# Attention with q/k norms, then a two-layer MLP: one swap of two VectorE steps, wider score groups in two units, one MLP item earlier in two others, two edits in the opening

## The chip, the cores and the metric

The kernel runs on one core of one Trainium2 chip. The metric is the device time of one execution in microseconds (us). A core has TensorE (PE in the profile, its weight loads PEld), VectorE (DVE), ScalarE (ACT), GpSimd (POOL) and SyncE (SP, which here only issues DMAs). Each engine runs its own instructions in the order in which the program recorded them; what ties them together are semaphores.

## The reference

q, k and v have 8 batches, 12 heads, 448 rows and 64 columns. The result goes through a two-layer MLP ("MoE" in the code) of 768 by 2048 and 2048 by 768.

```
q_n = q / sqrt(mean(q*q) + 1e-6) * g_q          # the same for k with g_k
scores = 1/8 * q_n @ k_n.T
attn = exp(scores - max(scores)); attn = attn / (sum(attn) + 1e-9)
x = (attn @ v), heads side by side: 3584 x 768
h = x @ w_in;  g = max(0.01*h, h);  out = g @ w_out
```

## The kernel before, in words

**Units.** The attention is cut into 24 units: unit u holds 4 heads of one batch, so a batch is three units. The 448 rows of a head are 7 tiles of 64, and the scores are computed transposed: for one of the seven steps t, four matmuls of 64x64 by 64x448 (L222) fill a pair of PSUM banks (a "slot"). ScalarE turns a slot into exponentials in one pass of 128x896 (`ex`, L242), which frees the slot. After the seven steps come attn @ v (`pv`, L398) and the column sums (`zcol`, L335).

**The shift in front of exp.** It comes from the first score tile of a unit: VectorE takes its maximum (L262), spreads it over a diagonal tile `dg` (L264), TensorE multiplies that by ones (L274, or L280 in the first units), VectorE reduces again (L275) and writes the bias `eb` (L285). Only then can the unit's first exp run.

**Four stages per unit.** In the main loop each unit has stages d = 0 to 3. Before, units 3 to 6 follow `STEPS`: one score step at d = 0 and two at each of the others. Units 7 to 21 follow `TRIPLES`: one at d = 0, three at d = 1, none at d = 2, three at d = 3 (`tripled(u)`, L780). Between the score groups TensorE runs items of the MLP out of one queue. How many are taken at each stage is written out by hand in `PLAN`, a string of four digits for each unit from unit 3 on (L774). An item is one tile of the first layer (`moe1`: 6 matmuls at L420, then ScalarE's activation L414, which frees its bank), half of a plain second-layer tile (`moe2`: 16 matmuls in two parts, L466, copied out by VectorE at L473), or one of seven products (`seven`, 8 matmuls each, L516). `seven` computes two output tiles with seven products instead of eight; its parts are merged by VectorE additions (L523).

**Who goes first on VectorE.** `fill` (L789) takes an item, then pops one job from the stage's list, and so on; `flush` runs what an item put off with `later`: copies, additions, and the `drop` of a bank. Jobs are steps that prepare later units: sums of squares (L180), 1/rms on ScalarE (L185, L186), the norm itself (`prep_norm`, two multiplications at L192, q and k), the transposition by DMA (L209), the scaling of the transposed q (L176), sums of weights for the seven products (L491). One exception is written out: in unit 12 no job follows the item that is marked `merges`.

**Banks.** PSUM has 8 banks. `aux` hands out one, `slot` a pair; as a rule the bank or pair that has been free the longest is taken (once all are shared, a single bank is taken first from a pair whose other half is in use), and its next matmul waits until the last reader of the previous use is done. Before unit 7 banks 0 to 3 are single ones and 4 to 7 make the two slots; from unit 7 on (`shared`, L1025) all eight are one pool.

**The opening.** Units 0 to 2 are written out line by line (L820 to L1021). TensorE runs matmuls without a use (`warm`, L817) where it would stand idle. Two places matter: 48 of them ahead of unit 0's transpositions (L832), and the bank `st[2]["pb"]`, held from the shift of unit 2 until after the transposition of q for unit 3 (`trn(3, 0)`, L986; `drop` at L988). `trn` transposes seven 128x128 tiles on TensorE (L204) into one single bank, and VectorE copies them out (L801 for q, L803 for k).

Of the kernel before, what the change touches and what calls it, by code (L numbers as in the profile page):

```python
# [18 lines left out]
def kernel(  # L19
# [18 lines left out]
    NU = B * NQ  # L38
# [25 lines left out]
    def aux():  # L64
        can = [i for i in free if mine(i)]
        if shared:
            can = [i for i in can[:-1] if i ^ 1 not in free] or can
        free.remove(can[0])
        return single[can[0]]
# [12 lines left out]
    def drop(tile_):  # L82
        for i in range(8):
            if tile_ is single[i]:
                assert i not in free
                free.append(i)
                return
        x = [i for i in range(4) if tile_ is double[i]][0]
        assert 2 * x not in free and 2 * x + 1 not in free
        free.extend((2 * x, 2 * x + 1))  # L90
# [42 lines left out]
    st = {}  # L133
# [33 lines left out]
    def prep_sq(u, c=ALL, tis=BOTH):  # L167
        for ti in tis:
            nc.scalar.activation(buf(u, f"sq{ti}")[:, :, c[0]:c[1]], raw[u][ti][:, :, c[0]:c[1]], AF.Square)  # L169
# [29 lines left out]
    def prep_tr(u, ti, copies):  # L199
        bank = aux()  # L200
        tp = as_tp(bank)
        for (lo, hi), copy in copies:
            for x in range(lo, hi):
                nc.tensor.transpose(tp[:, x, :], buf(u, "n16")[:, ti, x].rearrange("p a d -> p (a d)"), ident16)  # L204
            copy(buf(u, "qkT")[:, ti, lo:hi], tp[:, lo:hi], ti == 0)
        drop(bank)
# [25 lines left out]
    def ex(u, most=NS):  # L232
        s = st[u]
        if "et" not in s:
            s["et"] = epool.tile([P, NS, 2, S], FP16, tag="et", name="et")
        for t, sT in s["sT"][:most]:
            if isinstance(sT, list):
                for a in range(2):
                    nc.scalar.activation(s["et"][:, t, a], sT[a][:, 0:S], AF.Exp, bias=s["eb"], scale=1.0)  # L239
                    drop(sT[a])  # L240
            else:
                nc.scalar.activation(s["et"][:, t], sT[:, :, 0:S], AF.Exp, bias=s["eb"], scale=1.0)  # L242
                drop(sT)
        s["sT"] = s["sT"][most:]
# [189 lines left out]
    def store(pair, t, tile_, c, last):  # L434
        for y in range(2):
            n = 2 * t + (1 - y if t < 3 else y)
            b, grp = 2 * pair + n // NS, n % NS
            dst = out[b * S:(b + 1) * S, :].rearrange("(p t) m -> p t m", t=NS)
            eng = nc.scalar if last and y else nc.sync
            eng.dma_start(dst[:, grp, c], tile_[64 * y:64 * y + 64, c])  # L440
# [5 lines left out]
    def flush(keep=0):  # L446
        kept = [p for p in pend if keep and (p[0] in (s1, s2, s3, s4) or hasattr(p[0], "waits") or keep == 5 and hasattr(p[0], "copies"))]
        now = [p for p in pend if p not in kept]
        pend[:] = kept
        for fn, args in now:  # L450
            fn(*args)

    def out_tile():
        return opool.tile([P, DM], FP32, tag="ost", name="ost")
# [29 lines left out]
    def wblock(i, j):  # L484
        return wout16[:, HF * i:HF * i + HF, HC * j:HC * j + HC]
# [7 lines left out]
    def gblock(t, j):  # L493
        return gt[:, HF * j:HF * j + HF, ds(col(t), P)]
# [13 lines left out]
    def later(fn, *args):  # L508
        pend.append((fn, args))

    def seven(pair, tt, nxt=None, last=False, mixed=False):
        g = {}

        def mm(bank, a, b, first, fs=range(HF)):
            for f in fs:
                nc.tensor.matmul(bank[:, 0:HC], a[:, f], b[:, f], start=(first and f == 0), stop=(f == HF - 1), skip_group_check=not first)  # L516

        def bank(name):
            g[name] = aux()
            return g[name]  # L520

        def add(dst, src, name):
            nc.vector.tensor_tensor(dst, g[name][:, 0:HC], src, op=ALU.add)  # L523

        def put(i, c):
            store(pair, tt[i], g["o"][i], c, last)

        def i0():
            flush()
            g["o"] = (out_tile(), out_tile())  # L530
            ma = bank("ma")
            if mixed:
                mm(ma, gblock(tt[0], 0), wblock(0, 0), True, range(6))
                mm(bank("mb"), sa[:, 1], tw[:, 1], True, range(4))
            mm(ma, gblock(tt[0], 0), wblock(0, 0), True, range(6 if mixed else 0, HF))
            if mixed:
                mm(bank("mc"), sa[:, 0], tw[:, 0], True, range(4))
            later(lambda: nc.vector.tensor_copy(g["o"][1][:, L], g["ma"][:, 0:HC]))

        def i1():  # L540
            flush()
            mm(g["mb"] if mixed else bank("mb"), sa[:, 1], tw[:, 1], True, range(4 if mixed else 0, HF))
            later(lambda: add(g["o"][1][:, L], g["o"][1][:, L], "mb"))
            later(lambda: drop(g["mb"]))

        def i2():
            flush()
            mm(g["ma"], gblock(tt[0], 1), wblock(1, 0), False)
            later(lambda: nc.scalar.copy(g["o"][0][:, L], g["ma"][:, 0:HC]))
            later(lambda: drop(g["ma"]))  # L550
            if last:
                later(put, 0, L)

        def i3():
            flush()
            mm(g["mc"] if mixed else bank("mc"), sa[:, 0], tw[:, 0], True, range(4 if mixed else 0, HF))
            later(lambda: add(g["o"][1][:, R], g["o"][1][:, L], "mc"))
            if nxt:
                later(s1, nxt)

        def i4():
            flush()
            mm(bank("md"), sa[:, 2], tw[:, 2], True)
            later(lambda: add(g["o"][1][:, R], g["o"][1][:, R], "md"))
            if last:
                later(put, 1, R)

        i4.merges = True

        def i5():  # L570
            flush()
            mm(g["mc"], sa[:, 3], wblock(1, 1), False)
            if nxt:
                later(s2, nxt)
            later(lambda: add(g["o"][0][:, R], g["o"][1][:, L], "mc"))
            later(lambda: drop(g["mc"]))
            later(put, 0, R if last else LR)
            if nxt:
                later(s3, nxt)
                later(s4, nxt)  # L580

        def i6():
            flush()
            mm(g["md"], gblock(tt[1], 1), tw[:, 3], False)
            def end():
                add(g["o"][1][:, L], g["o"][1][:, L], "md")
                drop(g["md"])
                put(1, L if last else LR)

            end.waits = True  # L590
            later(end)

        return [i0, i1, i2, i3, i4, i5, i6]

    HK = KT // 2
# [133 lines left out]
    def push(b):  # L729
# [32 lines left out]
        else:  # L762
# [9 lines left out]
        queue.extend(items)  # L772

    PLAN = ("2122", "1222", "2112", "2122", "3232", "3322", "2322",  # L774
            "2322", "3232", "2222", "3323", "3232", "2322", "2322",
            "3232", "2222", "3323", "3232", "2322", "4356", "5232")
    STEPS = ((0,), (1, 2), (3, 4), (5, 6))
    TRIPLES = ((0,), (1, 2, 3), (), (4, 5, 6))

    def tripled(u):  # L780
        return 7 <= u < NU - 2

    def narrow(u):
        return 3 <= u < NU - 1
# [4 lines left out]
    def fill(u, d, jobs):  # L789
        for n in range(int(PLAN[u - 3][d])):  # L790
            fn = queue.pop(0)[1]
            fn()
            if jobs and not (d == 2 and u == 12 and hasattr(fn, "merges")):
                jobs.pop(0)()
        flush(keep=u if d == 3 and u < NU - 1 else 0)
        for job in jobs:
            job()
# [17 lines left out]
    def warm(n, bank):  # L815
        for x in range(n):
            nc.tensor.matmul(bank[:, P:2 * P], onesp, onesp, start=True, stop=True)  # L817

    with tc.manual_schedule():
# [7 lines left out]
        wbank = aux()  # L827
# [1 line left out]
        for a in range(2):  # L829
            nc.vector.scalar_tensor_tensor(gdup[:, a], grow[:, 0], 0.125, grow[:, 1], op0=ALU.mult, op1=ALU.mult)  # L830
        nc.tensor.matmul(gps[:, 0:1], gdup.rearrange("o a d -> o (a d)"), one32, start=True, stop=True)
        warm(48, wbank)  # L832
        prep_sq(0, CA, (0,))
        prep_sq(0, CB, (0,))
        prep_sq(0, ALL, (1,))
# [44 lines left out]
        def trn(u, ti, copy):  # L880
            prep_tr(u, ti, ((ALL, copy),))
# [101 lines left out]
        warm(12, st[2]["pb"])  # L983
        qk(2, (3,))
        ex(2)
        trn(3, 0, vcopy)  # L986
        warm(8, st[2]["pb"])
        drop(st[2]["pb"])  # L988
        trn(3, 1, vcopy)
        xmul(1)  # L990
        prep_ssq(4, ALL, (1,))
# [30 lines left out]

        for u in range(3, NU):
            for d in range(4):
                if u == 7 and d == 0:  # L1025
                    shared.append(u)
                if d > 0 or u > 3:
                    qk(u, (TRIPLES if tripled(u) else STEPS)[d])
# [22 lines left out]
                jobs = []  # L1051

                def job(fn, *args):
                    jobs.append(lambda: fn(*args))
# [69 lines left out]
        for i, more in enumerate((((xmul, NU - 1, (1,)), (x_sum, B - 1, 3), (x_sum, B - 1, 1)), ((x_sum, B - 1, 2), (x_sum, B - 1, 4)))):  # L1124
            c, fn = queue[i]
# [33 lines left out]
```

## Time and profile before

| | us |
|---|---|
| median of 3 runs (lowest, highest) | 412.99 (412.83, 414.09) |
| the profiled execution's own time | 412.78 |
| its span, from the first to the last instruction | 411.0 |
| TensorE busy in the span | 395.8 (96%) |
| VectorE busy | 308.7 (75%) |
| ScalarE busy | 299.6 (73%) |
| TensorE busy from 0 to 50 us | 41.4 of 50 |

The profile describes one execution. "Busy" counts the time in which at least one instruction of the engine is in work; matmuls are pipelined, so a matmul that waits a little between others can hide in a busy stretch. The chain that ended last is followed back from the last instruction: at each step to what released it. The view of waits sums, for each engine and line, how long it sat idle and who released it. The timeline lists start, duration, engine, line and operation in order of time, with a bracket for the idle time just before and its releaser. The granted TensorE clock was 0.998 over the span.

### The profile page before, as it was taken

Reading aid. Unit: us, or ns where it says so; the run is one execution under the profiler, and the core shown is the slowest. Engines: PE = TensorE matmul, PEld = TensorE weight load, DVE = VectorE, ACT = ScalarE, POOL = GpSimd, SP = SyncE. Lnnn points to the kernel's source line nnn. Section 1 sums busy time; section 2 is a strip of 40 time slices with the busy share of each in tenths; the row PEclk is TensorE's granted clock in tenths of the full one; section 3 lists DMA queues with packets and bytes.
Section 4 is the critical chain, followed back from the end, with each engine's and each line's share of the span. In section 5 each row is a group of like instructions: output and inputs, shape, how many; then the busy total and the mean of one; then the engine's idle time right before and its main releaser. Section 6 shows DMA issues by size and latency. Waiting matters only on the chain.

```text
span 411.0 us, 9411 instructions
## 1 busy us (share of the span) xinstructions
PE 395.8 (96%) x3840; PEld 223.8 (54%) x3840; DVE 308.7 (75%) x490; ACT 299.6 (73%) x470; POOL 69.3 (17%) x70
## 2 busy tenths in 40 slices
PE   8688999999999999999999999999999999999996
PEld 7455454455455544555454554555455557558963
DVE  5997789998888765867678766778578888657672
ACT  5998977677978599778877689868985667753600
POOL 1787332200020200020020200002011202000000
PEclk9999999999999999999999999999999999999999
DMA  6999999999565985578566996677652460032023
GB/s 201 263 238 253 236 235 239 229 194 195 140 155 97 242 216 105 148 195 179 147 157 69 224 203 132 156 147 193 176 98 46 121 154 15 10 77 77 2 52 102
DMA packets 72526, 62.87 MB, mean 153 GB/s; under 512 B 36388, under 2 KB 67620, under 8 KB 72484
## 3 DMA queue, kind: packets, MB, share of 16 engines
q1 hardware_dynamic: 61888, 50.08, 47.5%
q0 software_dynamic: 10272, 11.80, 18.4%
q8 instruction: 30, 0.49, 0.5%
q10 hardware_dynamic: 324, 0.39, 0.3%
q14 instruction: 12, 0.10, 0.1%
HBM read 45.61 MB, written 11.01 MB: 138 GB/s over the span
## 4 chain that ended last, share of the span: by engine, by line
PE 86%; DVE 6%; ACT 5%; issue 1%; DMA 1%; DVEq 0%; ACTq 0%
PE banks L420 28%; PE banks L516 22%; PE banks L222 9%; PE banks L466 8%; PE banks L398 7%; PE banks L648 6%; ACT et L242 3%; PE banks L335 3%; PE banks L817 2%; DVE n L192 1%; DMA out_dram<-ost 1%; PE banks L274 1%; PE banks L204 1%; DVE xt L407 1%; ACT et L239 1%
## 5 line engine op out<-in xcount | busy, mean ns | idle before, releaser
L242 ACT ACTIVATE et<-banks,eb 128x896 f16<-128x896 f32 x166 | 160.3, 1014 | 29.2 <-PE banks L222 16.9
L420 PE MATMUL banks<-xt,win 128*128 128x448 f16 x612 | 122.2, 353 | 0.0
L420 PEld LDWEIGHTS <-win 128*128 128x128 f16 x612 | 57.3, 98 | 55.8 <-issue 6.5
L414 ACT ACTIVATE gt<-banks 128x448 f16<-128x448 f32 x104 | 56.6, 564 | 6.3 <-PE banks L420 5.2
L222 PE MATMUL banks<-qkT 64*64 64x448 f16 x672 | 50.7, 362 | 4.5 <-ACT et L242 3.4
L180 DVE TENSOR_REDUCE ssq<-sq 128x14 f32<-128x896 f32 (+2 forms) x49 | 50.2, 1058 | 0.5 <-ACT sq L169 0.5
L516 PE MATMUL banks<-tw,sa 128*128 128x384 f16 x264 | 46.8, 326 | 2.0 <-DVE ost L523 2.0
L516 PEld LDWEIGHTS <-sa 128*128 128x128 f16 x352 | 33.5, 98 | 26.5 <-issue 5.5
L149 POOL DMA_DIRECT2D vt<-in_v_dram x24 | 17.9, 748 | 166.2 <-PE banks L398 165.8
L523 DVE TENSOR_TENSOR ost<-banks,ost 128x384 f32<-128x384 f32 x55 | 30.4, 553 | 16.1 <-PE banks L516 15.0
L222 PEld LDWEIGHTS <-qkT 64*64 64x64 f16 x672 | 17.8, 104 | 35.4 <-issue 28.6
L398 PE MATMUL banks<-et,vt 64*64 64x448 f16 x672 | 37.0, 349 | 0.1
L516 PEld LDWEIGHTS <-gt 128*128 128x128 f16 x264 | 25.5, 98 | 18.0 <-issue 1.4
L466 PE MATMUL banks<-wout,gt 128*128 128x384 f16 x192 | 34.1, 327 | 0.0
L376 POOL TENSOR_TENSOR xt<-x,rz 128x896 f16<-128x896 f32 x9 | 19.7, 2190 | 80.7 <-DMA rz<-zs 73.2
L262 DVE TENSOR_REDUCE banks<-banks 128x1 f32<-128x896 f32 x22 | 24.1, 1097 | 12.0 <-PE banks L222 8.8
L516 PE MATMUL banks<-wout,gt 128*128 128x384 f16 x176 | 32.4, 326 | 0.0
L350 ACT COPY x<-banks 128x896 f32<-128x896 f32 x16 | 14.5, 907 | 22.7 <-DVE banks L275 22.7
L192 DVE TENSOR_TENSOR n<-rq,rinv 128x896 f16<-128x896 f32 (+2 forms) x25 | 27.1, 1089 | 1.6 <-ACT rinv L186 1.6
L192 DVE TENSOR_TENSOR n<-rk,rinv 128x896 f16<-128x896 f32 (+2 forms) x26 | 27.5, 1065 | 0.0
L398 PEld LDWEIGHTS <-vt 64*64 64x64 f16 x672 | 20.3, 107 | 10.6 <-issue 0.4
L466 PEld LDWEIGHTS <-gt 128*128 128x128 f16 x192 | 17.7, 98 | 13.8 <-issue 3.2
(103 smaller groups left out, 468.5 us busy)
## 6 DMA issues: line engine op xcount, KB each, us to landing
rq<-in_q_dram SPq DMA_DIRECT2D x24, 448.0 KB, 4.1
rk<-in_k_dram SPq DMA_DIRECT2D x24, 448.0 KB, 4.6
out_dram<-ost SPq DMA_DIRECT2D x52, 192.0 KB, 3.5
rz<-zs SPq DMA_DIRECT2D x80, 112.0 KB, 2.3
vt<-in_v_dram POOLq DMA_DIRECT2D x24, 224.0 KB, 5.5
win<-in_moe_w_in_dram POOLq DMA_DIRECT2D x8, 384.0 KB, 15.1
wout<-in_moe_w_out_dram POOLq DMA_DIRECT2D x2, 1536.0 KB, 29.1
out_dram<-ost SPq DMA_DIRECT2D x4, 96.0 KB, 2.1
```

The lines of the kernel that those rows point to most:

```text
L180: nc.vector.tensor_reduce(buf(u, "ssq")[:, ti, :, c[0]:c[1]], buf(u, f"sq{ti}")[:, :, c[0]:c[1]], axis=AXL.X, op=ALU.add)
L192: nc.vector.tensor_tensor(buf(u, "n16")[:, ti, c[0]:c[1]].rearrange("p s a d -> p a s d"), src[:, :, c[0]:c[1]], buf(u, "rinv")[:, ti, :, ...
L222: nc.tensor.matmul(banks[a][64 * r:64 * r + 64, 0:S].rearrange("p (t x) -> p t x", t=NS), kT(u, r, a, t), qT(u, r, a), start=True, stop=True)
L242: nc.scalar.activation(s["et"][:, t], sT[:, :, 0:S], AF.Exp, bias=s["eb"], scale=1.0)
L262: nc.vector.tensor_reduce(s["spare"][:, 511:512], sT[:, :, 0:S], axis=AXL.XY, op=ALU.max)
L398: nc.tensor.matmul(s["pv"][r][64 * a:64 * a + 64, 0:S], vts[u % NV][64 * r:64 * r + 64, a, t], s["et"][64 * r:64 * r + 64, t, a], start=(t ...
L414: nc.scalar.activation(dst, src, AF.Prelu, bias=0.0, scale=1.0, alpha=0.01)
L420: nc.tensor.matmul(hps[:, 0:S], win16[:, kt // 2, kt % 2, ts(ft, P)], xt[:, kt // 2, kt % 2], start=(kt == 0), stop=(kt == KT - 1))
L466: nc.tensor.matmul(op2[:, 0:HC], gt[:, ft, ds(col(t), P)], wout16[:, ft, ds(HC * half, HC)], start=(i == 0), stop=(i == FT - 1))
L516: nc.tensor.matmul(bank[:, 0:HC], a[:, f], b[:, f], start=(first and f == 0), stop=(f == HF - 1), skip_group_check=not first)
L523: nc.vector.tensor_tensor(dst, g[name][:, 0:HC], src, op=ALU.add)
L648: nc.tensor.matmul(bank[:, HX * i:HX * i + HX].rearrange("p (t x) -> p t x", t=NS), w, x[:, kt], start=start, stop=(kt == HK - 1), skip_gr ...
```

## The change

- `seven`'s item `i1` gets a mark, `merged`. In stage 2 of units 14 and 20 no job is popped behind it, so the additions that `i2`'s `flush` runs come ahead of the norm of q. On VectorE one L523 and one L192 change places in each of the two units; on the other engines nothing moves for it.
- `tripled` holds from unit 5 instead of unit 7, and all eight banks are shared from unit 5. The scores of units 5 and 6 come in groups of 1, 3 and 3 steps instead of 1, 2, 2 and 2.
- In units 10 and 16 `PLAN` is 3222 instead of 2322: one `moe1` item, 6 matmuls and an activation, moves from behind the first group of three to ahead of it.
- In the opening, 42 `warm` matmuls instead of 48, and `drop(st[2]["pb"])` ahead of `trn(3, 0)`. The second transposition, `trn(3, 1)`, so gets the bank that `pb` held, and not the one that `trn(3, 0)` has just used.

```diff
             later(lambda: add(g["o"][1][:, L], g["o"][1][:, L], "mb"))
             later(lambda: drop(g["mb"]))
+
+        i1.merged = True
...
     PLAN = ("2122", "1222", "2112", "2122", "3232", "3322", "2322",
-            "2322", "3232", "2222", "3323", "3232", "2322", "2322",
+            "3222", "3232", "2222", "3323", "3232", "2322", "3222",
             "3232", "2222", "3323", "3232", "2322", "4356", "5232")
...
     def tripled(u):
-        return 7 <= u < NU - 2
+        return 5 <= u < NU - 2
...
-            if jobs and not (d == 2 and u == 12 and hasattr(fn, "merges")):
+            if jobs and not (d == 2 and (u == 12 and hasattr(fn, "merges") or u in (14, 20) and hasattr(fn, "merged"))):
...
-        warm(48, wbank)
+        warm(42, wbank)
...
         ex(2)
+        drop(st[2]["pb"])
         trn(3, 0, vcopy)
         warm(8, st[2]["pb"])
-        drop(st[2]["pb"])
         trn(3, 1, vcopy)
...
-                if u == 7 and d == 0:
+                if u == 5 and d == 0:
                     shared.append(u)
```

The instruction counts of VectorE, ScalarE, GpSimd and SyncE stay the same, and the orders of GpSimd and SyncE too; TensorE has six matmuls fewer, with their weight loads.

## The prediction

> **What bounds the kernel now.** I read the page's busy rows first: TensorE is busy for 395.8 of 411.0 us, VectorE for 308.7, ScalarE for 299.6. So nearly the whole span is one queue of matmuls, and only what moves TensorE's own idle time, or a wait hidden in its busy rows, can move the end. In windows of 10 us, TensorE stands idle for 8.6 us between 0 and 50, for 0.43 between 70 and 80, 0.98 each in 210 to 220 and 310 to 320, 0.08 each in 140 to 150 and 240 to 250; the rest is in the last 10 us. The chain that ended last says the same: 86% TensorE, and from 45 us on almost nothing else. Next I read whom TensorE waits for (us in total, times, longest):
>
> ```profile
> PE banks L222 <- ACT et L242: 3.4, 8, 0.7
> PE banks L516 <- DVE ost L523: 2.0, 2, 1.0
> ...
> PE banks L204 <- DVE qkT L801: 0.3, 1, 0.3
> ```
>
> The second line is two waits of 1.0 us for one addition; the third is in the opening. Then I went to each place in the timeline.
>
> **Merge ahead of the norm, units 14 and 20.** Unit 14, stages 2 and 3:
>
> ```profile
> 215.38 0.76 PE L222 MATMUL banks<-qkT 64*64 64x448 f16 x12
> ...
> 215.53 1.08 DVE L192 TENSOR_TENSOR n<-rq,rinv 128x896 f16<-128x896 f32 x1
> ...
> 216.53 0.54 DVE L523 TENSOR_TENSOR ost<-banks,ost 128x384 f32<-128x384 f32 x1
> ...
> 217.12 2.76 PE L516 MATMUL banks<-tw,sa 128*128 128x384 f16 x16 [0.98 <-DVE ost L523]
> ```
>
> TensorE is done with the scores at 216.14 and needs a bank that the addition L523 still reads; that stands on VectorE behind the norm of q. Swapped, L523 would start at 215.53 and end near 216.07. Unit 8 has the same items in these stages and already has that order:
>
> ```profile
> 121.80 0.76 PE L222 MATMUL banks<-qkT 64*64 64x448 f16 x12
> ...
> 121.95 0.55 DVE L523 TENSOR_TENSOR ost<-banks,ost 128x384 f32<-128x384 f32 x1
> ...
> 122.42 1.08 DVE L192 TENSOR_TENSOR n<-rq,rinv 128x896 f16<-128x896 f32 x1
> ...
> 122.55 2.76 PE L516 MATMUL banks<-tw,sa 128*128 128x384 f16 x16
> ```
>
> No bracket on the last line: no wait. From the first L516 of the stage to the next unit's first score it takes 125.24 - 117.81 = 7.43 us in unit 8, and 219.81 - 211.38 = 8.43 in unit 14. What gets later: the norms of q and k end at the old clock time (218.1), and so does the transposition by DMA behind them, while TensorE is 0.98 earlier. In unit 8 that is covered: the next unit's `dg` is ready at 127.36, its matmul L274 runs at 127.47 without a wait, and the scaling L176 has no DMA wait. If that cover of 0.1 us failed, the following unit would give back at most the norm's 1.08, so each swap lies between -0.1 and +0.98. I take 0.98 twice, **1.96**, by the row of unit 8.
>
> **One item ahead in units 10 and 16.** The first group of three in unit 10 (unit 16 has the same rows at 240.36):
>
> ```profile
> 145.79 1.21 PE L222 MATMUL banks<-qkT 64*64 64x448 f16 x12
> 146.01 0.56 ACT L414 ACTIVATE gt<-banks 128x448 f16<-128x448 f32 x1
> ```
>
> From here to the next matmul it is 1.14 us (146.93); elsewhere twelve score matmuls take 0.69 on the chain. The third slot holds the bank of the first MLP item, whose activation L414 ends at 146.57: a wait of 0.45 that the busy row hides. With six more matmuls ahead (1.13 us) the group starts at 146.9 and asks for that slot at 147.4, so nothing waits. Its exps start behind one more L414, 147.6 instead of 147.14, and end near 150.9; the second group asks for their slots only at 152.05. So 0.45 each, if VectorE is ready for the next unit. In unit 10 it has 1.41 us to spare at L262. In unit 16 `dg` is ready at 252.28, and TensorE's L274 would come at 252.04 instead of 252.49: it waits, and 0.17 is left. There the norm was held up by 2.0 us for a DMA (rz), in unit 10 by 0.71, so I take 0.3 between 0.17 and 0.45. Sum **0.75**, bounds 0 (a third item's activation lands in the way) and 0.90.
>
> **Fewer warm matmuls.** The 48 end where the transposition of q starts (8.32). Its input, the first norm, runs from 7.16 for 0.68, so it is ready at 7.84. The last seven warm matmuls take 0.55 with 0.22 for one, 55 ns from start to start; six less are 0.33, to 7.99, still behind the norm. ScalarE's copy starts at 8.47 instead of 8.80 and the first scores at 9.68 instead of 10.01; VectorE's copy of k's first tile, ready at 9.52, is in time. From 10 us on the chain alternates between engines without slack, so **0.33** passes on; the input of unit 1 lands at 9.0 to 9.4 (issue 5.42, 3.6 to landing), ahead of its use at 9.5. One step would not follow: VectorE's L180 at 22.0 needs a GpSimd square that ends at 21.79 and is held by DMAs; ScalarE's chain, which ends last there, does not pass through it. Bounds: 0 and 0.33.
>
> [...]
>
> **The bank dropped early.** The two transpositions for unit 3:
>
> ```profile
> 34.97 0.68 DVE L801 TENSOR_SCALAR qkT<-banks,gcol 128x896 f16<-128x896 f16 x1 [0.63 <-PE banks L204]
> ...
> 35.71 0.55 PE L204 MATMUL banks<-ident,n 128*128 128x128 f16 x7 [0.33 <-DVE qkT L801]
> ...
> 36.30 0.62 DVE L803 COPY qkT<-banks 128x896 f16<-128x896 f16 x1 [0.64 <-PE banks L204]
> ```
>
> The second waits for the copy of the first because both use one bank. With `pb`'s bank it follows the 8 warm matmuls at 35.26 and ends at 35.83; L803 starts then instead of at 36.30, and L407, the next link of the chain, 0.46 earlier. To 43.8 us the chain is L407, L398, exp, L428, all behind it. **0.46**, bounds 0 and 0.64 (VectorE's idle time there).
>
> **Groups of three in units 5 and 6.** On the chain eight score matmuls cost 0.50, twelve 0.69; sixteen L466 take 2.60, and 0.1 more on the way back to scores. Unit 5 now, from 72.66 to 80.30: 7.64 us with one exp wait of 0.43. After: 0.69 + 2.70 + 0.69 + 2.70 = 6.78, so 0.86 less. The slots are in time: the group asks for its third one, exp 3's, at 76.4, and that exp ends near 75.9; exp 6 ends near 80.2 and is needed at 80.8. Unit 6: 8.16 now, 7.94 after. Together 1.08. But VectorE does not follow:
>
> ```profile
> 79.75 1.08 DVE L192 TENSOR_TENSOR n<-rk,rinv 128x896 f16<-128x896 f32 x1
> 80.75 1.09 DVE L262 TENSOR_REDUCE banks<-banks 128x1 f32<-128x896 f32 x1
> ```
>
> From 74.34 to 85.02 it has no idle time. `dg` stays at 82.16, so L274 moves from 82.66 only to 82.2 (0.46 gained), and the copy L348, which frees a slot, still ends at 85.02, so unit 6's first group starts at 85.07 instead of 85.42 (0.35). With unit 6's 0.22 that is 0.57, and unit 7's `dg` at 95.51 holds it to 0.46 if VectorE gains nothing. I take **0.5**. Bounds: 1.08 above; below, -0.95, one exp, if a third slot comes one exp late.
>
> **Sum.** 1.96 + 0.75 + 0.33 + 0.46 + 0.5 = 4.0. Against the profiled execution's own 412.78 (span 411.0, 1.8 around it; the median of the runs is 412.99, 0.2 above): 412.78 - 4.0 = **408.8 us**.
>
> **Rivals.**
> - *VectorE holds what the opening and units 5 and 6 save.* For: no idle time on it from 57.4 to 72.1 and 74.3 to 85.0, and at 69.83 L274 has only 0.1 us of slack behind `dg` (69.71). Against: those stretches begin with waits for TensorE. Then only the swaps and the moved items count: 412.78 - 2.7 = 410.1.
> - *The swap moves the wait.* The next unit's start waits for the norm, and half of the 1.96 comes back: 409.8; with the first rival 411.1. Against: unit 8.
> [...]
> - *It doesn't do what it says:* excluded for the swaps, which stand in the recorded order of VectorE.
>
> **Numbers.** Forecast 0.66 (407.9 to 409.5), VectorE 0.20, the swap's wait moved 0.09, slower 0.03, something else near no change 0.02. All gains at their upper bounds give 412.78 - 4.9 = 407.9; the first rival is at 410.1. With 0.2 on both sides, by which the profiled execution and the median differ, the range is 407.7 to 410.3; it leaves out some 0.15. A measurement of this kernel tells about 0.3% (1.2 us) from no change: faster 0.93, same 0.04, slower 0.03.
>
> **What would show it.** Right: no wait for L523 at the two L516 rows; L222 x12 near 0.76 instead of 1.21 in units 10 and 16; L204 without a wait for L801; no L222 wait for an exp in unit 5; a new short wait of L274 for `dg` in unit 6. Wrong: a longer one there, a new wait of L274 in units 15 and 21, or a warm pitch of 112 ns after 8 us.

## The result and the profile after

The changed kernel took 411.71 us in the median (22 runs, 409.12 to 416.49), the kernel before 413.06 in the same comparison (22 runs, 412.27 to 416.88). The ratio of the means is 0.9955, 95% interval 0.9933 to 0.9976: faster by 0.45% against a forecast of 1.0%, and outside its range. (This interval, and those below, leave out the few executions that lie over 1.5% above the fastest of the same kernel.) What stands out is the spread: most runs of before lie within 2 us, those of the changed kernel are strewn over 7, and the lowest, 409.12, is almost the forecast.

The profiled execution took 413.38 us (span 411.5), 0.6 more than before's. It shows a bad case in full. Line numbers of the changed kernel are two higher from L545 on; those below it are the same. The whole run's waits of TensorE (us in total, times, longest):

```profile
PE banks L222 <- ACT et L242: 3.0, 7, 0.7
PE banks L420 <- DVE ost L473: 2.0, 1, 2.0
PE banks L274 <- DVE dg L264: 1.7, 3, 0.8
```

The two waits for L523 are gone, and so is L204's for the copy. In their place stands a new one of 2.0 us, for a copy (L473) that nobody touched. Unit 14 in the timeline:

```profile
218.01 0.76 PE L222 MATMUL banks<-qkT 64*64 64x448 f16 x12
...
218.16 0.55 DVE L523 TENSOR_TENSOR ost<-banks,ost 128x384 f32<-128x384 f32 x1
...
218.76 2.76 PE L516 MATMUL banks<-tw,sa 128*128 128x384 f16 x16
```

No bracket on L516: the swap works as forecast. So does the bank in the opening (k's copy starts at 35.81 instead of 36.30), the item ahead in unit 10 (the first twelve L222 show 0.76 instead of 1.21), and, on TensorE, the groups of three in unit 5: the next unit's first score comes at 78.90 instead of 80.23, and L274 waits 0.67 for `dg`, as foretold. The rows, in order of time:

```profile
35.81 0.62 DVE L805 COPY qkT<-banks 128x896 f16<-128x896 f16 x1 [0.15 <-PE banks L204]
...
78.90 0.38 PE L222 MATMUL banks<-qkT 64*64 64x448 f16 x4
...
82.24 0.22 PE L274 MATMUL banks<-dg,onesp 128*128 128x64 f16 x2 [0.67 <-DVE dg L264]
...
150.00 0.76 PE L222 MATMUL banks<-qkT 64*64 64x448 f16 x12
```

The loss comes right behind. The places where unit 6 issues its transfers, in the timeline of the changed kernel:

```profile
80.92 1.32 SPq L209 DMA_TRANSPOSE qkT<-n  x1
81.09 0.76 POOL L149 DMA_DIRECT2D vt<-in_v_dram  x1 [3.52 <-PE banks L398]
...
90.16 0.46 DVE L176 TENSOR_SCALAR qkT<-qkT,gcol 128x896 f16<-128x896 f16 x1 [3.57 <-DMA qkT<-n]
```

and in that of the kernel before:

```profile
80.89 1.33 SPq L209 DMA_TRANSPOSE qkT<-n  x1
...
82.26 0.76 POOL L149 DMA_DIRECT2D vt<-in_v_dram  x1 [4.71 <-PE banks L398]
...
86.87 0.45 DVE L176 TENSOR_SCALAR qkT<-qkT,gcol 128x896 f16<-128x896 f16 x1
```

The transposition of unit 7's q and k starts at the same time in both, but took 9.2 us to land instead of 4.4. What moved is the line between: GpSimd's load of V for unit 9 may overwrite its buffer when the attn @ v matmuls (L398) of unit 5 are done, and these come 1.2 us earlier because TensorE is ahead. In the trace's single packets the transposition is 1792 packets of 256 bytes and the V load 256 of 896. Before, 7 of the V packets start within the transposition (82.1 to 84.8); after, 232 do, and it takes from 82.1 to 88.7. The windows show what the transfers moved (columns: the stretch and its length, busy time of TensorE, its weight loads, VectorE, ScalarE and GpSimd, granted clock, DMA share, GB/s), changed kernel first, then before:

```profile
82.00:84.00 2.00, 1.76 (x13) 1.11 (x13) 1.97 (x6) 0.00 (x0) 0.00 (x0) 1.00 1.06 86
84.00:86.00 2.00, 1.95 (x21) 1.05 (x20) 1.89 (x4) 1.82 (x4) 0.00 (x0) 1.00 1.26 61
```

```profile
82.00:84.00 2.00, 2.00 (x38) 1.33 (x31) 1.97 (x6) 0.00 (x0) 0.76 (x1) 1.00 1.14 120
84.00:86.00 2.00, 2.00 (x19) 0.91 (x17) 1.50 (x3) 1.79 (x4) 0.00 (x0) 1.00 1.15 178
```

DMA is "busy" throughout, but from 84 to 86 us, with both transfers in flight, it moves 61 instead of 178 GB/s. The amount of data doesn't explain that: in these 2 us only 15 of V's packets start, beside 426 of the transposition's; most of the 232 follow after 86. VectorE, in order, stands 3.57 us at L176; behind it are two reductions, the copy L473 (for which TensorE then waits 2.0) and the norms of unit 8.

From here on I follow a kernel by the start of L262 in each unit, less that in before's profile (us):

| unit | 5 | 6 | 7 | 10 | 11 | 14 | 16 | 17 | 20 | 22 |
|---|---|---|---|---|---|---|---|---|---|---|
| changed kernel | -0.48 | +0.03 | +3.23 | +3.08 | +2.63 | +2.64 | +1.64 | +1.18 | +1.19 | +0.19 |

The opening gains 0.48, units 5 and 6 lose 3.7 (0.5 of it in unit 5, where L176 waits 0.73 for the transposition of unit 6 instead of 0.22), each moved item gives 0.45 (10 to 11, 16 to 17), each swap 1.0 (14 to 16, 20 to 22). A loss of 0.36 in unit 22 shows in some profiles and not in others; it stays unexplained.

### The profile page after: what moved, and what is told of

Its sections match the earlier page's. It is cut to its first block, busy times and chain, and to the rows that moved or that the text cites. A ratio compares the mean times of both kernels' runs of the same rounds, so it can differ in the third digit from the quotient of the medians.

```text
span 411.5 us, 9401 instructions
## 1 busy us (share of the span) xinstructions
PE 395.4 (96%) x3834; PEld 223.8 (54%) x3834; DVE 308.6 (75%) x490; ACT 298.9 (73%) x470; POOL 69.1 (17%) x70
## 4 chain that ended last, share of the span: by engine, by line
PE 85%; DVE 7%; ACT 3%; DMA 2%; issue 1%; SPq 0%; DVEq 0%
PE banks L420 28%; PE banks L516 25%; PE banks L222 9%; PE banks L650 6%; PE banks L398 6%; PE banks L466 5%; PE banks L335 2%; PE banks L819 2%; DMA qkT<-n 2%; ACT et L242 1%; DVE n L192 1%; DVE banks L262 1%; DVE ssq L180 1%; DMA rz<-zs 1%; PE banks L274 1%
## 5 line engine op out<-in xcount | busy, mean ns | idle before, releaser
L222 PE MATMUL banks<-qkT 64*64 64x448 f16 x672 | 49.7, 361 | 3.9 <-ACT et L242 3.0
L516 PE MATMUL banks<-tw,sa 128*128 128x384 f16 x264 | 46.8, 326 | 0.0
L516 PEld LDWEIGHTS <-sa 128*128 128x128 f16 x352 | 33.5, 98 | 24.6 <-issue 3.6
L523 DVE TENSOR_TENSOR ost<-banks,ost 128x384 f32<-128x384 f32 x55 | 30.4, 553 | 14.7 <-PE banks L516 14.1
L398 PE MATMUL banks<-et,vt 64*64 64x448 f16 x672 | 37.0, 349 | 0.1
L222 PEld LDWEIGHTS <-qkT 64*64 64x64 f16 x672 | 17.4, 104 | 33.8 <-issue 26.4
L516 PEld LDWEIGHTS <-gt 128*128 128x128 f16 x264 | 25.5, 98 | 18.0 <-issue 1.4
L262 DVE TENSOR_REDUCE banks<-banks 128x1 f32<-128x896 f32 x22 | 24.1, 1097 | 13.1 <-PE banks L222 9.4
L376 POOL TENSOR_TENSOR xt<-x,rz 128x896 f16<-128x896 f32 x9 | 19.6, 2175 | 80.3 <-DMA rz<-zs 72.7
L516 PE MATMUL banks<-wout,gt 128*128 128x384 f16 x176 | 32.4, 326 | 0.0
L192 DVE TENSOR_TENSOR n<-rq,rinv 128x896 f16<-128x896 f32 (+2 forms) x25 | 27.2, 1092 | 2.1 <-ACT rinv L186 2.1
L192 DVE TENSOR_TENSOR n<-rk,rinv 128x896 f16<-128x896 f32 (+2 forms) x26 | 27.6, 1067 | 0.0
L398 PEld LDWEIGHTS <-vt 64*64 64x64 f16 x672 | 20.4, 107 | 10.7 <-issue 0.6
```

Source lines behind the costliest of these rows:

```text
L192: nc.vector.tensor_tensor(buf(u, "n16")[:, ti, c[0]:c[1]].rearrange("p s a d -> p a s d"), src[:, :, c[0]:c[1]], buf(u, "rinv")[:, ti, :, ...
L222: nc.tensor.matmul(banks[a][64 * r:64 * r + 64, 0:S].rearrange("p (t x) -> p t x", t=NS), kT(u, r, a, t), qT(u, r, a), start=True, stop=True)
L262: nc.vector.tensor_reduce(s["spare"][:, 511:512], sT[:, :, 0:S], axis=AXL.XY, op=ALU.max)
L398: nc.tensor.matmul(s["pv"][r][64 * a:64 * a + 64, 0:S], vts[u % NV][64 * r:64 * r + 64, a, t], s["et"][64 * r:64 * r + 64, t, a], start=(t ...
```

## The experiments

**Theory A:** the groups of three bring the V load into the transposition, and that is what costs. **Rival B:** VectorE is too full in units 5 and 6 with the groups of three, load or no load. **Rival C:** the other edits deliver less than one profile shows. "Before" is the median of before's runs taken beside them; the ratio is that of means, with its 95% interval.

| run | median (low to high, runs) | before | ratio |
|---|---|---|---|
| e1_no_triples | 410.20 (408.88 to 415.08, 9) | 413.11 | 0.9935 (0.9911 to 0.9958) |
| e2_triples_only | 413.10 (412.18 to 417.35, 12) | 413.11 | 1.0003 (0.9975 to 1.0031) |
| e3_swaps_only | 411.23 (410.64 to 411.68, 6) | 413.11 | 0.9944 (0.9930 to 0.9958) |
| e4_v_held | 412.29 (411.25 to 413.50, 12) | 413.11 | 0.9972 (0.9953 to 0.9991) |
| e5_items_only | 412.34 (411.77 to 413.17, 12) | 413.27 | 0.9978 (0.9967 to 0.9988) |
| e6_drop_only | 412.69 (412.16 to 416.64, 12) | 413.27 | 1.0004 (0.9979 to 1.0030) |
| e7_warm_only | 413.31 (412.47 to 418.14, 12) | 413.07 | 1.0013 (0.9989 to 1.0038) |
| e8_no_v9 | 409.69 (409.46 to 410.70, 6) | 413.27 | 0.9914 (0.9899 to 0.9928) |
| e9_v_gated | 409.82 (409.12 to 410.99, 6) | 413.27 | 0.9916 (0.9899 to 0.9933) |
| e10_gated_no_triples | 410.11 (409.84 to 411.07, 6) | 413.07 | 0.9925 (0.9905 to 0.9946) |
| e11_v_early | 414.04 (412.66 to 415.39, 12) | 413.07 | 1.0021 (1.0003 to 1.0038) |
| e12_v_both | 409.08 (408.37 to 410.01, 6) | 413.07 | 0.9897 (0.9875 to 0.9918) |
| e13_q_in_place_of_v | 410.49 (410.22 to 410.85, 5) | 413.07 | 0.9936 (0.9923 to 0.9950) |
| e14_q_behind_norm | 411.19 (410.21 to 412.52, 10) | 413.37 | 0.9941 (0.9915 to 0.9967) |
| e15_q_free | 409.93 (409.05 to 413.04, 9) | 413.37 | 0.9904 (0.9872 to 0.9936) |

**e1: the change without the groups of three.** `tripled` and `shared` from unit 7 again.

> The changed kernel with triples and the shared pool from unit 7 on, as before; every other edit kept. Theory A (the triples of unit 5 bring the V load of unit 6, on POOL's queue, 1.2 us forward into the transposition of unit 7's qkT; in the changed kernel's profile 232 of the load's 256 packets fall into it, and the VectorE scaling L176 waits 3.57 us): swaps 1.96, items 0.8, bank 0.49 and warm 0 to 0.33 are left, so 3.2 to 3.6 us below before, 409.5 to 409.9, with runs as close together as before's. Theory B (VectorE is too full in units 5 and 6 with the triples, with or without the load): the same. Theory C (another edit delivers less than the trace shows, or the runs spread for another reason): about 411.7, with runs as far apart as those of the changed kernel.

2.9 below before, so rival C falls: most of what the trace promised is there. But three of nine runs still lie at 412.6 to 415.1, which I had not expected. In its profile the V load is issued 1.46 us after the transposition, and nothing goes wrong.

**e2: the groups of three alone.** `tripled` and `shared` from unit 5 in the kernel before.

> The kernel before with the triples and the shared pool from unit 5 on, and nothing else of the change. Theories A and B: the mean of the changed kernel is 1.4 us below before although its other edits are worth 3.2 or more, so this edit alone costs 1.9 us in the median: 415.0, with single runs from 412.2 (no collision: 0.8 gained) to 416.4 (the profiled case: 3.3 lost). By the prediction's sum 412.3; theory C: 412.3 to 413.

Nothing in the median, but spread over 5 us. The profiled run, 415.95, has the same picture as the changed kernel: V issued 0.17 us behind the transposition, 221 packets in it, 9.0 us to landing, L176 waiting 3.35. It doesn't tell A from B.

**e3, e5: the swaps alone, the moved items alone.**

> The kernel before with the two swaps alone (units 14 and 20). All theories that take the trace at its word: 2 x 0.98 = 1.96 us below before, 411.0 to 411.2. Theory C, if it is the swaps that deliver less in most executions: 412 to 413.

> The kernel before with the MoE item moved ahead in units 10 and 16, alone. By the trace of the changed kernel both stalls of 0.45 us are gone: 0.75 to 0.9 below before, 412.2 to 412.4, and its runs as close together as before's. If its runs spread as those of the changed kernel without triples did (409 to 413), the items have to do with that.

1.88 and 0.93 by the medians, and 2 x 1.0 and 0.45 + 0.46 in the profiles; both sets of runs are close together. The swaps and the items deliver what the prediction said, and bring no new spread.

**e4: V held until the transposition has landed, units 5 to 7.** In front of `load_v(u + 3)`:

```diff
+    if u in (5, 6, 7):
+        nc.gpsimd.tensor_copy(vts[(u + 3) % NV][:, 1, NS - 1, D - 1:D], buf(u + 1, "qkT")[:, 1, NS - 1, P - 1:P])
```

> The changed kernel, with the V loads of units 5, 6 and 7 held on POOL's queue until the transposition under way has landed (a one-element copy from qkT into the tile that the load then overwrites; V is needed 25 us later). Theory A: the transposition of unit 7 lands in 4.0 to 4.6 us again, L176 does not wait 3.6 us, the triples keep their 0.5 to 0.8, and the time is 408.6 to 409.4 with runs close together. Theory B: 411.7, far apart, as the changed kernel. If the load only moves onto another DMA that is waited for (rz of L366 at 85.9 us): 409.5 to 411, with the wait at L376.

The transposition of unit 7 landed in time (packets 82.3 to 84.7, none of V's among them), and L176 didn't wait. Still 412.29: in unit 6 the load now ran at 87.3 to 89.9, into the transfers of rz (one over the column sums, L366), and L376 waited 1.34 us for them; in unit 5 the hold pushed GpSimd's squares onto VectorE's L491, which took 3.00 us instead of the 1.66 that it takes at this place in before. The wait was moved, as in the third case of the expectation, and by the squares a second time, which I had not foreseen. This profile is of the fastest of the twelve runs (411.25), so it need not show all that the others lose. Alone e4 left rival B standing.

**e8, e9: take the load away, or issue it where it was.** e8 leaves out `load_v(9)`; e9 holds it for unit 6's `dg`:

```diff
+    if u == 6:
+        nc.gpsimd.tensor_copy(vts[(u + 3) % NV][:, 1, NS - 1, D - 1:D], st[u]["dg"][:, P - 1:P])
     load_v(u + 3)
```

> The changed kernel without the V load of unit 6 (V of unit 9): that unit's output is computed from the V left in the buffer, so it leaves one load out. Theory A (that load's packets in the transposition cost the time): the transposition of unit 7 lands in 4.0 to 4.6 us, neither L176 nor L376 waits over 0.3 us in unit 6, and the whole change is then worth swaps 1.96 + items 0.8 + bank 0.49 + triples 0.3 = 3.5 us: 409.0 to 409.9, mostly close together. Theory B (VectorE is too full with the triples, load or no load): 411 or more, with the delay at L262 of unit 7 still there.

> The changed kernel, with the V load of unit 6 alone held on POOL's queue by a one-element copy from unit 6's dg (L264, written at 82.2 us), so that it is issued where it was in the kernel before (82.26 us; 81.09 in the changed kernel): 1.2 us later. Theory A: the load falls again between the transposition (through at 84.8) and the rz transfers (from 87.7), as in the kernel before: 409.0 to 409.9. If DMA traffic near it is too dense anyway: as the changed kernel or as the load held for longer, 411 to 412.3.

Both at 409.7 to 409.8, with all runs within 2 us. The timeline of e9:

```profile
81.21 1.32 SPq L209 DMA_TRANSPOSE qkT<-n  x1
...
83.08 0.76 POOL L149 DMA_DIRECT2D vt<-in_v_dram  x1 [0.30 <-POOL vt L1071]
...
86.79 0.45 DVE L176 TENSOR_SCALAR qkT<-qkT,gcol 128x896 f16<-128x896 f16 x1
```

Everything of the change is in this kernel; only one load is issued *later* (1.9 us behind the transposition, before 1.4), and its median is 1.9 us below that of the changed kernel (1.6 by the ratios of the means). Rival B falls: VectorE does the same work in both.

**e11: the same collision in the kernel before.** No groups of three, nothing of the change:

```diff
+    if u == 6:
+        gate(u + 1)
+        load_v(u + 2)
-    if u + 3 < NU:
+    elif u + 3 < NU:
         load_v(u + 3)
```

> The kernel before, with one thing moved: in unit 6 the V load is issued about 1.2 us earlier, at 81.1 us (behind a one-element copy that waits for the norm of unit 7). To be free to go early it loads unit 8's V once more, the same bytes into the same buffer, in place of unit 9's, which is left out (unit 9's output then comes from old V). No triples and nothing else of the change. Theory A (the load's place in time against the transposition is what costs): the transposition of unit 7 lands 2 to 5 us later than its 4.4 us, L176 waits, and the median goes up by 1 to 3 us, 414 to 416, with single runs up to 417. Rival (the triples themselves do it, the load only goes along): 412.3 to 413.3, as before.

1.0 us slower, at the low end of what theory A expected, with an interval above 1. In its timeline:

```profile
81.08 2.11 SPq L209 DMA_TRANSPOSE qkT<-n  x1
...
81.31 0.76 POOL L149 DMA_DIRECT2D vt<-in_v_dram  x1
...
88.78 0.45 DVE L176 TENSOR_SCALAR qkT<-qkT,gcol 128x896 f16<-128x896 f16 x1 [2.10 <-DMA qkT<-n]
```

The time between these two issues in unit 6 sorts the profiles: 0.17 to 0.23 us (changed kernel, e2, e11) gives 7.7 to 9.2 us to landing; 1.2 and more (before, e1, e3 to e7, e9, e10, e12) gives 4.2 to 4.8. This holds for unit 6 alone: in unit 7 the changed kernel has 0.48 and before 1.91, and L176 waits 1.57 and 1.14. There V's packets start at 100.7 in the changed kernel, when the transposition (98.2 to 101.0) is nearly through.

**e10: e9 without the groups of three.**

> The changed kernel with the V load of unit 6 gated by dg and without the triples and the shared pool in units 5 and 6. By the sum of what the single edits gave (swaps 1.9, items 0.9, bank 0.5): 3.3 below before, 409.8, close together: the single runs at 412.6 to 415.1 that the same kernel showed without the gate should be gone, if they too were this load in the transposition. Against 409.8 with the triples: equal within 0.3 says that the triples gain next to nothing even without the collision, since VectorE has no idle time in unit 5 and 6 to give; 410.3 says that they are worth the prediction's 0.5.

410.11, and none of its six runs strays as three of e1's nine did. That fits the same load, with a margin of 1.4 us that isn't always enough, but it isn't shown: six runs are few, no profile caught a stray of e1, and the one that e15's profile caught lies in unit 5, which e10 leaves as it was. The groups of three are worth 0.3 by these medians (410.11 - 409.82), with intervals that overlap widely: neither 0 nor the 0.5 of the prediction is excluded.

**e6, e7: the two edits in the opening, each alone.**

> The kernel before with the bank dropped early in the opening, alone. By the trace of the changed kernel 0.49 us at unit 3; the prediction had 0.46: 412.6. If the transposition of unit 6 lands at the same time however early it is issued (74.3 us in both profiles), VectorE gives the gain back in unit 5: 413.0.

> The kernel before with 42 in place of 48 warm matmuls in the opening, alone. The prediction took 6 x 55 ns = 0.33 us; in the changed kernel's profile the 42 took as long as the 48 had, at 104 to 112 ns each up to 6.8 us, and nothing came of it. 0.33: 412.8; nothing: 413.1. The runs' own spread may not tell these apart; the profile does, at the first transposition.

e6: 0.58 in the median, but three of twelve runs at 415.7 to 416.6 eat it up in the mean; its profile caught none of these. e7: nothing. In e7's timeline the 42 matmuls end at 7.30 and the transposition then waits for the norm:

```profile
4.78 2.52 PE L817 MATMUL banks<-onesp 128*128 128x128 f16 x42
...
8.04 0.90 PE L853 MATMUL banks<-ident,n 128*128 128x128 f16 x8 [0.73 <-DVE n L192]
```

In e3 and e5, all 48 take 2.85 us, end by 7.7, and the transposition waits for the norm as well (0.23 and 0.24). Before's profile, where 48 took 3.34 and ended last, was not the usual case.

**e12: both V loads out of the way.** e9, and in unit 5 the V load behind GpSimd's first square:

```diff
+    if u == 5:
+        prep_sqp(u + 3, (0,))
     load_v(u + 3)
     if u < 6:
-        prep_sqp(u + 3)
+        prep_sqp(u + 3, (1,) if u == 5 else (0, 1))
```

> The changed kernel with the V load of unit 6 gated by dg, and in unit 5 the V load behind POOL's first square, 1.9 us later, so that its packets come when the transposition of unit 6 is through (73.0 to 73.5 us) and not in its last part. Theory A at its other place: L176 of unit 6's qkT, which waited 1.43 us with the gate alone and 0.73 in the changed kernel, waits 0 to 0.3, the opening's gain is no longer lost in unit 5, and 0.3 to 0.8 comes off 409.8: 409.0 to 409.5. If that wait comes from the q and k loads still under way at 69 to 71 us: 409.8 again.

409.08, 1.0% below before: the best of all, and the size that was forecast for the change alone. In unit 5, 16 instead of 76 V packets start within the transposition and L176 waits 0.67 instead of 1.43, not 0 to 0.3. The transposition's packets took longer there all the same (4.7 us against 3.9), in both with some 140 packets of the q and k loads among them; what got shorter is the time from its last packet to L176 (0.5 against 1.7). So in unit 5 V's packets are not the only ones in the way. Its interval overlaps that of e9, so whether the second move adds to the first isn't settled.

**e13 to e15: what makes the mixture slow?** All leave out V of unit 9 as e8 does, and load q of unit 9 once more from ScalarE's queue, released at three times. The diff is e13's, where the load is held until unit 6's `dg`; in e14 the copy reads unit 7's `n16` in place of `dg`, and e15 has no copy:

```diff
+    if u == 6 and d == 0:
+        t = raw[9][0]
+        nc.scalar.copy(t[:, 1, NS - 1, D - 1:D], st[u]["dg"][:, P - 1:P])
+        nc.scalar.dma_start(t.rearrange("p a t d -> p a (t d)"), rows(q, 9))
```

> [...] Theory S (any packets mixed in with the transposition's slow it): the transposition of unit 7 again lands 2 to 5 us later than its 4.4 us, L176 waits 1 to 4 us, 411 to 413. [...]

> As the run with q in place of V (V of unit 9 left out, q of unit 9 loaded once more from ScalarE's queue), but held only until the norm of unit 7 is done, which also releases the transposition: there the load's first packets came at 85.2 us, when the transposition (82.8 to 86.1) was almost through, so it told nothing. Now the packets should begin some 1.2 us after the transposition's first ones; in the changed kernel the V load's came 1.8 us after them. Theory S (any packets mixed in slow it): the transposition lands 2 to 5 us later than 4.4, L176 waits. [...]

> The same without any hold: the load goes out as soon as ScalarE is done with unit 5 (about 80.8 us) and the tile's first load has landed, so its packets should begin with the transposition's or ahead of them. Theory S: 2 to 5 us later, or, if all its packets get in ahead of the transposition's, some 2 us later (448 KB at the 200 to 260 GB/s that the profile shows). [...]

e13 told nothing: the load's packets came at 85.6, when the transposition (to 86.1) was almost through. e14 hit it:

```profile
81.05 1.32 SPq L209 DMA_TRANSPOSE qkT<-n  x1
...
81.28 0.41 ACTq L1049 DMA_DIRECT2D rq<-in_q_dram  x1
...
88.63 0.46 DVE L176 TENSOR_SCALAR qkT<-qkT,gcol 128x896 f16<-128x896 f16 x1 [1.91 <-DMA qkT<-n]
```

From 84 to 86 us DMA moved 46 GB/s, and L176 waited 1.91: theory S. GpSimd isn't needed for it; a load from another queue does the same. e15's load was through before the transposition began, which then landed in time. But its profiled run, 413.04, caught a collision in unit 5, of the transposition of unit 6 with the V load of unit 8:

```profile
67.95 3.58 SPq L209 DMA_TRANSPOSE qkT<-n  x1
...
69.40 0.76 POOL L149 DMA_DIRECT2D vt<-in_v_dram  x1 [7.05 <-PE banks L398]
...
77.35 0.45 DVE L176 TENSOR_SCALAR qkT<-qkT,gcol 128x896 f16<-128x896 f16 x1 [3.65 <-DMA qkT<-n]
```

185 V packets start within the transposition, and 128 of the q and k loads that are still under way; this profile doesn't separate the two. The distance of 1.45 us is the same as in before's unit 5 (68.36 and 69.81, 65 packets, a wait of 0.22): there the outcome varies from run to run.

## Why the prediction was wrong

- **Groups of three, units 5 and 6: the step that failed.** Taken at +0.5, with -0.95 at worst. The matmuls did what was worked out, and `dg` held L274 as said. But the bounds asked only for VectorE and the exp slots, and no rival has a transfer in it. The step also moves attn @ v, and with it the release of a V load on GpSimd's queue; no wait was charged to L176, which the trace of before shows in unit 6 without one. With that load kept behind the transposition (e9) the change is worth 0.84%, 3.5 us, with 409.82 inside the range. So 1.9 of the 2.9 us between the forecast and the measured 411.71 are this one transfer. The profile shows it at 3.6; that other executions pay anything from nothing to that is read from the spread of the runs alone.
- **Without the collision** the 0.5 may have been right. They give 0.3 by the medians of e9 and e10, within the noise; in e8's profile, where L176 waits in neither unit 5 nor 6, it takes 57.11 us from the L262 of unit 5 to that of unit 9, in before's 57.66. The first rival, VectorE holding what TensorE saves, isn't shown.
- **Fewer warm matmuls: failed too, by 0.33.** Its working rests on a profile in which the warm matmuls ended last. In e3 and e5 the norm does, and in e7 the cut only lengthens the wait for it. The changed kernel's own 42 took 3.35 us, as long as before's 48, because their pace changed later: from 107 to 56 ns from start to start at 7.0 us, in before at 6.2, in e3, e5 and e7 by 4.9. In before's trace the slow pace lasts from 1.16 to 6.2, 5.1 us. The granted clock reads 1.00 in every microsecond from 0 to 10 in the profiles of both kernels, so what sets the pace isn't shown. Whether the cut pays in executions with a late change, no run shows.
- **The swaps: right**, 1.0 each in the profiles for 0.98, 1.88 together in e3. The rival that the wait only moves has nothing for it.
- **The moved items: right**, a little low: 0.45 and 0.46 for 0.45 and 0.3. In unit 16 nothing of the 0.45 went back to `dg`.
- **The bank: right in the profile** at unit 3 (0.48 for 0.46), but the changed kernel's profile gives it back in unit 5, at L176; in the runs of e6 it drowns in strays.
- **A low granted clock in the opening** does occur, but no run shows it to be the change's doing. It shows in e3, which has none of the opening's edits:

```profile
28.00:30.00 2.00, 2.00 (x25) 1.56 (x25) 1.43 (x6) 1.49 (x2) 1.72 (x2) 0.54 1.08 258
30.00:32.00 2.00, 2.00 (x32) 1.00 (x28) 2.00 (x4) 1.84 (x5) 0.89 (x1) 0.61 1.12 262
```

The granted clock (third column from the end) is 0.54 from 28 to 30 us and 0.61 from 30 to 32, with 1.00 in the 2 us ahead and behind, and from the first L262 to unit 3's it takes 0.8 us longer than in before's profile. In the changed kernel's profile that clock is 1.00 from 8 to 44 us, and the warm matmuls there stand 56 ns apart (12 in 0.84 us). The 112 ns that the prediction names as a sign of being wrong is the mean of the first 32 warm matmuls in before's trace (3.59 us for all); from start to start they stand 107 ns apart. The 0.03 for a slower kernel was the author's estimate; no run shows the edits slowing the kernel through the clock.

## What to carry to other kernels

When an engine gets ahead, list the transfers that its semaphores release, on every queue, even where the order of no queue changes; ask what else is in flight at the new time and who waits for that. A wait that the trace shows at zero is no proof of slack: look how close the nearest other transfer is (here 1.4 us), and check the spread of the runs before taking one profile as the kernel. If a transfer has time to spare, tie it to something that comes at the right moment.

## What the runs showed of the hardware

- A transposition by DMA (1792 packets of 256 bytes) and a load in flight together can take longer than one after the other: alone the transposition's packets go through in 2.3 us (the changed kernel's next but one, 112.6 to 114.9) or 3.2 (e8, the one of unit 7 without the V load) and the V load's in about 2 (115.3 to 117.5); together they took 7.0 (82.1 to 89.2, with rz's transfers beside them from 87 on), the transposition 6.6 of it, and from 84 to 86 us DMA moved 61 GB/s (46 in e14). Loads from GpSimd's queue and from ScalarE's both reach into a transposition from SyncE's: in the changed kernel 232 of V's packets start within it; in e14 q's load, issued at 81.28 us, took 6.4 to land (3.5 in e15, where it was through first), and the transposition, issued at 81.05, held L176 until 88.63. Why the mixture moves so little was not found; in e8 the transposition stalls for 1 us (22 packets from 82.5 to 83.5) with no V load at all, so the V load isn't all that slows it.
- VectorE's subtraction L491 (128x1536, fp16) took 0.95 us alone (before, at 86.00), 1.66 beside the end of a GpSimd square (before, at 76.69) and 3.00 in e4, where GpSimd's squares ran from 74.32 to 77.65 and it from 75.47 to 78.47. A hold on GpSimd's queue isn't free if work stands behind it.
